# A conv and leaky-ReLU MLP on one core: the conv cut to 512-token blocks in three jobs a step, x cast on ScalarE, one transpose slot per block, and the first loads and casts set out anew

## Chip, cores and metric

One core of one Trainium2 chip. The metric is the device time of the kernel in microseconds; each time is one execution.

## What is computed

```python
# x (8, 4096, 192), weight (8 heads, 7 taps), w_in (192, 2048), w_out (2048, 192)
w = softmax(weight, axis=-1)
x_pad = zeros of 6 tokens in front of x, along the sequence
conv[b, s, h, g] = sum over k of w[h, k] * x_pad[b, s + k, h, g]   # 8 heads of 24 channels
a = conv.reshape(32768, 192)
h = a @ w_in
g = maximum(0.01 * h, h)
out = g @ w_out            # (32768, 192), float32
```

A causal depthwise convolution with seven taps, then two matrix products with a leaky ReLU between them.

## The kernel before

**Tiling.** Two sequences are worked at once, as two halves `e` of 64 partitions; the 192 channels are three chunks `c` of 64. A block is 512 tokens of both sequences, so there are 4 x 8 = 32 blocks. Each block passes through these stages: `load_x` (two DMAs on SP's queue, L72, 384 KB each, into one of three x_nat buffers), `cast_x` (float32 to bfloat16 on DVE, L85, two casts of 768 elements per partition), `transpose_x` (24 TensorE transposes of 64 rows, L101, into two PSUM tiles ptr0 and ptr1), `evac_x` (two DVE copies into the transposed sequence `xt`, L117), the conv (DVE, L134 for the first tap and L140 for the other six, per chunk), `mm1` (L242, six matmuls of 64 rows for each of 16 slices f of d_ff, the two sequences in the two row halves of the array), the leaky ReLU on ACT (Prelu, L249, 1024 elements), `mm2` (L260) and `evac_o` (a DVE copy out of PSUM, L303, and for every second one an output DMA on SP's queue, L306).

**Order.** The order of every engine's instructions is written out by hand. The main loop goes over 33 blocks and 8 steps j in each. A step of a block holds mm1 for two slices f with their Prelus, and the mm2 work of one 128-token output tile n of the block before (`n = (blk - 1) * 8 + j`): 16 matmuls of the upper row half for tile n, and 16 of the lower row half that run LAG = 24 matmuls, a step and a half, behind. So tile n-2 is finished in the middle of step n, and `evac_o(n-2)` is the first DVE work of that step. The lower half of a tile starts only behind the first Prelu of its step (`seal`). The last tiles are done with whole 128-row matmuls.

**PSUM.** `ph` has two slots of two banks. The tag `po` has four slots of one bank: the output sums take them, and the two transpose tiles ptr0 and ptr1 too, so a transpose needs an emptied sum's slot, and the next sum may get a transpose tile's slot.

**The conv.** It is made for units of two blocks (1024 tokens): 21 jobs of 1024 elements for a unit, spread over the 16 steps before it is needed; the first unit is done in pieces of 512.

**Preparation of later x.** In blocks 0 and 1, two blocks are prepared in each; from block 2 on, `prep(blk + 4, j, 1)` puts the load of blk+6 and the casts of blk+4 into step 1, and the transposes, one conv job and the xt copies into step 2:

```python
        if j == at:
            if blk + 2 < NBLK:
                load_x(blk + 2)
            cast_x(blk)
        if j == at + 1:
            transpose_x(blk)
            run_jobs(1)
            evac_x(blk)
```

**The start.** x of blocks 0 and 1 is loaded on SP's queue; the tap weights `wk` come in 20 small DMAs, half on POOL's queue and half on ACT's (L160); w_in (L171, two DMAs of 1536 KB, the same data for both partition halves) and w_out (L176, 1536 KB) follow on POOL's queue. 60 warm-up matmuls of 128 columns (L183) run early. The softmax of the taps (L191 to L206) comes ahead of the casts, transposes and copies of block 0 on DVE, then the conv of block 0. ACT casts w_in in four quarters (L221), then w_out (L226), and only then does its first Prelu.

Of the kernel before, what the change touches and what calls it, by code (L numbers as in the profile page):

```python
# [9 lines left out]
FP32 = mybir.dt.float32  # L10
BF16 = mybir.dt.bfloat16
# [3 lines left out]
def kernel(  # L15
# [8 lines left out]
    nc = tc.nc  # L24

    B, S, D = x.shape
    H, K = weight.shape
    Din, F = moe_w_in.shape
    GRP = D // H
# [8 lines left out]
    SUB = ST // 128  # L38
    NFC = F // 128
    NB = S // ST  # L40
    UB = 2
    UT = UB * ST
    NU = NB // UB
    NRP = B // 2
    NBLK = NRP * NB
    NUNIT = NRP * NU
    STEPS = 8
    FPS = NFC // STEPS

    const_pool = ctx.enter_context(tc.tile_pool(name="const", bufs=1))  # L50
# [11 lines left out]
    out_rows = out.rearrange("(r s) d -> r s d", r=B)  # L62


    x_nat = {}
    xt = {}

    def load_x(blk):
        rp, st = divmod(blk, NB)
# [10 lines left out]
    x_bf = {}  # L80

    def cast_x(blk):
        t = xb_pool.tile([128, SUB, NCH, 2, CH], BF16, name="x_bf")
        for e in range(2):
            nc.vector.tensor_copy(  # L85
                out=t[:, :, :, e, :],
                in_=x_nat[blk][:, e, :, :].rearrange("p s (c k) -> p s c k", c=NCH),
            )
        x_bf[blk] = t

    ptr = {}

    def transpose_x(blk):

# [10 lines left out]
                    )  # L105
        ptr[blk] = ts

    def evac_x(blk):
        rp, st = divmod(blk, NB)
        if st == 0:  # L110
            xt[rp] = xt_pool.tile([128, NCH, HALO + S], BF16, name="xt")
            nc.vector.memset(xt[rp][:, :, 0:HALO], 0.0)
        dst = xt[rp][:, :, HALO + st * ST : HALO + (st + 1) * ST].rearrange(
            "p c (s i k) -> p i s c k", s=SUB, i=2
        )
        for i, t in enumerate(ptr.pop(blk)):
            nc.vector.tensor_copy(out=dst[:, i], in_=t)  # L117


    yt = {}  # L120

    def conv_jobs(unit, pieces):
        rp, u = divmod(unit, NU)
        y = yt_pool.tile([128, NCH, UT], BF16, name="yt")
        yt[unit] = y
        jobs = []
        for o, n in pieces:
            for c in range(NCH):
                for k in range(K):
                    src = xt[rp][:, c, BASE + k + u * UT + o : BASE + k + u * UT + o + n]  # L130
                    dst = y[:, c, o : o + n]
                    if k == 0:
                        jobs.append(
                            lambda s=src, d=dst, c=c: nc.vector.tensor_scalar_mul(  # L134
                                d, s, wk[:, c, 0:1]
                            )
                        )
                    else:
                        jobs.append(
                            lambda s=src, d=dst, c=c, k=k: nc.vector.scalar_tensor_tensor(  # L140
                                out=d, in0=s, scalar=wk[:, c, k : k + 1], in1=d,
                                op0=mybir.AluOpType.mult, op1=mybir.AluOpType.add,
                            )
                        )
        return jobs

    load_x(0)
    load_x(1)


    wk = const_pool.tile([128, NCH, K], FP32, name="wk")
    for e in range(2):
        for c in range(NCH):
            lo = c * CH
            while lo < (c + 1) * CH:
                h = lo // GRP
                hi = min((h + 1) * GRP, (c + 1) * CH)
                p = e * CH + lo - c * CH
                eng = nc.gpsimd if e == 0 else nc.scalar
                eng.dma_start(  # L160
                    out=wk[p : p + hi - lo, c, :],
                    in_=weight[h : h + 1, :].to_broadcast((hi - lo, K)),
                )
                lo = hi
# [5 lines left out]
    for e in range(2):  # L170
        nc.gpsimd.dma_start(  # L171
            out=w_stage[e * CH : (e + 1) * CH, :, :],
            in_=moe_w_in.rearrange("(c p) f -> p c f", p=CH),
        )
    wo_stage = g_pool.tile([128, NFC, D], FP32, name="wo_stage", tag="g")
    nc.gpsimd.dma_start(  # L176
        out=wo_stage, in_=moe_w_out.rearrange("(c p) d -> p c d", p=128)
    )


    wa = psum_h.tile([128, 2, ST], FP32, name="warm", tag="ph")
    for i in range(60):
        nc.tensor.matmul(  # L183
            out=wa[:, 0, 0:128], lhsT=ident, rhs=ident,
            start=(i == 0), stop=(i == 59),
        )


    nmax = const_pool.tile([128, NCH], FP32)
    ssum = const_pool.tile([128, NCH], FP32)  # L190
    nc.vector.tensor_reduce(  # L191
        out=nmax, in_=wk, axis=mybir.AxisListType.X,
        op=mybir.AluOpType.max, negate=True,
    )
    for c in range(NCH):
        nc.scalar.activation(  # L196
            out=wk[:, c, :], in_=wk[:, c, :], func=mybir.ActivationFunctionType.Exp,
            bias=nmax[:, c : c + 1], scale=1.0,
        )
# [5 lines left out]
    for c in range(NCH):  # L205
        nc.vector.tensor_scalar_mul(wk[:, c, :], wk[:, c, :], ssum[:, c : c + 1])  # L206


    cast_x(0)
    transpose_x(0)  # L210
    evac_x(0)
    first = conv_jobs(0, [(0, ST), (ST, ST)])
    for job in first[: NCH * K]:
        job()
    cast_x(1)
    transpose_x(1)
    evac_x(1)

    w_in = const_pool.tile([128, NCH, F], BF16)
    for q in range(4):  # L220
        nc.scalar.copy(  # L221
            out=w_in[:, :, q * (F // 4) : (q + 1) * (F // 4)],
            in_=w_stage[:, :, q * (F // 4) : (q + 1) * (F // 4)],
        )
    w_out = const_pool.tile([128, NFC, D], BF16)
    nc.scalar.copy(out=w_out, in_=wo_stage)  # L226

    load_x(2)
    load_x(3)


    g = {}
    po = {}

    def mm1(blk, f):
        unit, ub = divmod(blk, UB)
        y = yt[unit]
        ph = psum_h.tile([128, 2, ST], FP32, name="ph", tag="ph")
        for c in range(NCH):
            for e in range(2):  # L240
# [1 line left out]
                nc.tensor.matmul(  # L242
                    out=ph[:, e, :],
                    lhsT=w_in[ps, c, f * 128 : (f + 1) * 128],
                    rhs=y[ps, c, ub * ST : (ub + 1) * ST],
                    start=(c == 0),
                    stop=(c == NCH - 1),
                )
# [29 lines left out]
    def mm2(n):  # L278
# [11 lines left out]
        if n >= LAST:  # L290
            for fc in range(NFC):
                mm2_one(None, n, fc)
            if n < NBLK * STEPS - 1:
                evac_o(n)

    def evac_o(n):
        blk, j = divmod(n, STEPS)
# [10 lines left out]
                in_=osb.pop(n // 2),  # L308
            )

    LAG = NFC + NFC // 2
    LAST = (NBLK - 1) * STEPS - 1
    osb = {}
    seal = {}
    jobs = list(first[NCH * K :])

    def prep(blk, j, at):
        if not blk < NBLK:
            return
        if j == at:  # L320
            if blk + 2 < NBLK:
                load_x(blk + 2)
            cast_x(blk)
        if j == at + 1:
            transpose_x(blk)
            run_jobs(1)
            evac_x(blk)

    def run_jobs(n):
        for _ in range(min(n, len(jobs))):  # L330
            jobs.pop(0)()

    for blk in range(NBLK + 1):
        unit, ub = divmod(blk, UB)
        if blk < NBLK:
            g[blk] = g_pool.tile([128, NFC, 2, ST], BF16, name="g", tag="g")
        for j in range(STEPS):
            n = (blk - 1) * STEPS + j
            if blk < NBLK:
# [3 lines left out]
                        seal[n] = act.ins.name  # L343
            if n >= 0:
                mm2(n)
            if blk == 0:
                prep(2, j, 0)
                prep(3, j, 4)
            elif blk == 1:
                prep(4, j, 0)  # L350
                prep(5, j, 4)
            else:
                prep(blk + 4, j, 1)
            if ub == 0 and j == (7 if blk == 0 else 0) and unit + 1 < NUNIT:
                jobs += conv_jobs(unit + 1, [(0, UT)])

            left = (7 - j) if blk == 0 and j < 7 else (UB - ub) * STEPS - j
            run_jobs(-(-len(jobs) // left))
    evac_o(NBLK * STEPS - 1)


# [28 lines left out]
```

## Time and profile before

| | |
|---|---|
| median of 3 runs | 757.04 us (756.85 to 759.33) |
| profiled execution | 757.87 us |
| its span | 756.1 us |
| TensorE matmul busy (PE) | 700.1 us, 93% |
| weight loads (PEld) | 565.5 us, 75% |
| VectorE (DVE) | 520.3 us, 69% |
| ScalarE (ACT) | 506.6 us, 67% |
| GpSimd (POOL) | 8.5 us |
| mean granted TensorE clock | 0.981 |
| HBM read, written | 29.90 MB, 25.17 MB |

The span is the time from the first to the last instruction; the execution's own time is 1.77 us more. The busy share is an average over a start, a long steady part and an end. PE counts a matmul from its start to its modelled end, so back-to-back matmuls overlap in it. In the rows shown below, `x12` counts instructions, and a name in brackets behind an idle time is what ended it; a group's row ends with its busy time, the mean nanoseconds of one instruction, and the idle time ahead of it with what ended that.

### The profile page before, as it was taken

What the parts mean: (1) busy time and instruction counts of PE and PEld (TensorE: products, weight loads), DVE (VectorE), ACT (ScalarE), POOL (GpSimd) and SP (SyncE); (2) the same over time, 40 slices, a digit from 0 to 9 for tenths busy, and PEclk for the clock granted to TensorE, in tenths of its full rate; (3) what the DMA queues carried; (4) which work ended last, traced back from release to release, by engine and by line L of the source; (5) the groups of instructions that cost most, each with busy time, mean ns of one, the idle gap of its engine ahead of it and who ended that gap; (6) DMA issues with size and microseconds to landing.
All of it is one profiled execution on the core that took longest, in us unless ns stands there. A gap on an engine that the chain in (4) does not pass through costs nothing.

```text
span 756.1 us, 25743 instructions
## 1 busy us (share of the span) xinstructions
PE 700.1 (93%) x11948; PEld 565.5 (75%) x11948; DVE 520.3 (69%) x752; ACT 506.6 (67%) x521; POOL 8.5 (1%) x19
## 2 busy tenths in 40 slices
PE   3178799999999999999999999999999999999997
PEld 3036578787877878787787878778787877888887
DVE  3979876867767687776768687676868677675112
ACT  1485567676777777676776767777676767777771
POOL 4000000000000000000000000000000000000000
PEclk9589999999999999999999999999999999999999
DMA  8921212222221222222122222221222211111112
GB/s 202 265 77 40 66 56 86 75 86 75 76 84 35 86 75 86 75 86 75 46 73 85 75 75 86 75 66 53 86 75 86 75 34 43 44 33 44 33 44 64
DMA packets 70131, 56.71 MB, mean 75 GB/s; under 512 B 3752, under 2 KB 69304, under 8 KB 69640
## 3 DMA queue, kind: packets, MB, share of 16 engines
q1 hardware_dynamic: 68608, 50.34, 22.0%
q0 software_dynamic: 1104, 4.73, 2.7%
q8 instruction: 93, 1.52, 0.8%
q14 instruction: 14, 0.11, 0.1%
q10 hardware_dynamic: 312, 0.01, 0.0%
HBM read 29.90 MB, written 25.17 MB: 73 GB/s over the span
## 4 chain that ended last, share of the span: by engine, by line
PE 81%; DVE 11%; DMA 3%; issue 3%; ACT 1%; POOL 0%; ACTq 0%; POOLq 0%
PE po L260 40%; PE ph L242 39%; DVE yt L140 7%; DMA w_stage<-in_moe_w_in_dram 3%; DVE x_bf L85 2%; PE ptr L101 2%; DVE o_sb L303 1%; ACT w_in L221 1%; DMA wk<-in_weight_dram 1%; DVE xt L117 1%; ACT w_out L226 0%; ACT g L249 0%; DVE yt L134 0%; POOL wk L160 0%; POOL w_stage L171 0%
## 5 line engine op out<-in xcount | busy, mean ns | idle before, releaser
L249 ACT ACTIVATE g<-ph 128x1024 bf16<-128x1024 f32 x512 | 496.4, 1021 | 204.9 <-PE ph L242 204.9
L260 PEld LDWEIGHTS <-g 64*128 64x128 bf16 (+1 forms) x8048 | 364.1, 94 | 47.2 <-issue 4.2
L242 PE MATMUL ph<-yt,w_in 64*128 64x512 bf16 x3072 | 388.7, 379 | 10.0 <-ACT g L249 4.9
L260 PE MATMUL po<-w_out,g 64*128 64x192 bf16 (+1 forms) x8048 | 391.6, 243 | 3.1 <-DVE xt L117 3.0
L140 DVE SCALAR_TENSOR_TENSOR yt<-xt,wk,yt 128x1024 bf16<-128x1024 bf16 (+1 forms) x306 | 371.8, 1215 | 3.5
L242 PEld LDWEIGHTS <-w_in 64*128 64x128 bf16 x3072 | 195.9, 95 | 97.0 <-issue 17.8
L303 DVE COPY o_sb<-po 128x192 f32<-128x192 f32 x256 | 90.9, 355 | 209.8 <-PE po L260 209.8
L101 PE MATMUL ptr<-ident,x_bf 64*128 64x64 bf16 x768 | 20.4, 193 | 30.3 <-DVE x_bf L85 17.3
L101 PEld LDWEIGHTS <-x_bf 64*128 64x128 bf16 x768 | 17.4, 97 | 33.6 <-DVE x_bf L85 17.9
L117 DVE COPY xt<-ptr 128x768 bf16<-128x768 bf16 x64 | 32.4, 547 | 7.0 <-PE ptr L101 7.0
L85 DVE CAST x_bf<-x_nat 128x768 bf16<-128x768 f32 x64 | 32.6, 551 | 0.0
L134 DVE TENSOR_SCALAR yt<-xt,wk 128x1024 bf16<-128x1024 bf16 (+1 forms) x51 | 23.6, 462 | 0.0
L221 ACT CAST w_in<-w_stage 128x1536 bf16<-128x1536 f32 x4 | 5.6, 1468 | 18.1 <-DMA w_stage<-in_moe_w_in_dram 18.1
L183 PE MATMUL warm<-ident 128*128 128x128 bf16 x60 | 6.2, 301 | 8.3 <-POOL ident masks.py:199 8.3
L183 PEld LDWEIGHTS <-ident 128*128 128x128 bf16 x60 | 6.0, 144 | 8.3 <-POOL ident masks.py:199 8.3
L191 DVE TENSOR_REDUCE nmax<-wk 128x3 f32<-128x21 f32 x1 | 0.2, 174 | 10.6 <-DMA wk<-in_weight_dram 10.6
L196 ACT ACT_TABLE_LOAD x1 | 1.3, 1283 | 7.6 <-DMA wk<-in_weight_dram 7.6
L160 POOL DMA_DIRECT2D wk<-in_weight_dram x10 | 5.3, 539 | 1.9 <-DMA wk<-in_weight_dram 1.1
L226 ACT CAST w_out<-wo_stage 128x3072 bf16<-128x3072 f32 x1 | 2.7, 2747 | 0.0
L196 ACT ACTIVATE wk<-wk,nmax 128x7 f32<-128x7 f32 x3 | 0.8, 301 | 2.0 <-DVE nmax L191 2.0
L171 POOL DMA_DIRECT2D w_stage<-in_moe_w_in_dram x2 | 1.3, 646 | 0.0
L176 POOL DMA_DIRECT2D wo_stage<-in_moe_w_out_dram x1 | 1.2, 1196 | 0.0
(11 smaller groups left out, 2.2 us busy)
## 6 DMA issues: line engine op xcount, KB each, us to landing
x_nat<-in_x_dram SPq DMA_DIRECT2D x64, 384.0 KB, 4.4
out_dram<-o_sb SPq DMA_DIRECT2D x128, 192.0 KB, 2.0
w_stage<-in_moe_w_in_dram POOLq DMA_DIRECT2D x2, 1536.0 KB, 17.0
wo_stage<-in_moe_w_out_dram POOLq DMA_DIRECT2D x1, 1536.0 KB, 25.5
wk<-in_weight_dram ACTq DMA_DIRECT2D x6, 0.7 KB
wk<-in_weight_dram POOLq DMA_DIRECT2D x6, 0.7 KB, 4.5
wk<-in_weight_dram ACTq DMA_DIRECT2D x2, 0.4 KB, 4.3
wk<-in_weight_dram ACTq DMA_DIRECT2D x2, 0.2 KB
```

Of the source, the lines that this page charges most:

```text
L85: nc.vector.tensor_copy(out=t[:, :, :, e, :], in_=x_nat[blk][:, e, :, :].rearrange("p s (c k) -> p s c k", c=NCH),)
L101: nc.tensor.transpose(out=ts[i][:, s, c, :], in_=x_bf[blk][ps, s, c, :, :].rearrange("p e k -> p (e k)"), identity=ident[ps, ps],)
L117: nc.vector.tensor_copy(out=dst[:, i], in_=t)
L134: lambda s=src, d=dst, c=c: nc.vector.tensor_scalar_mul(d, s, wk[:, c, 0:1])
L140: lambda s=src, d=dst, c=c, k=k: nc.vector.scalar_tensor_tensor(out=d, in0=s, scalar=wk[:, c, k : k + 1], in1=d, op0=mybir.AluOpType.mult, ...
L160: eng.dma_start(out=wk[p : p + hi - lo, c, :], in_=weight[h : h + 1, :].to_broadcast((hi - lo, K)),)
L183: nc.tensor.matmul(out=wa[:, 0, 0:128], lhsT=ident, rhs=ident, start=(i == 0), stop=(i == 59),)
L221: nc.scalar.copy(out=w_in[:, :, q * (F // 4) : (q + 1) * (F // 4)], in_=w_stage[:, :, q * (F // 4) : (q + 1) * (F // 4)],)
L242: nc.tensor.matmul(out=ph[:, e, :], lhsT=w_in[ps, c, f * 128 : (f + 1) * 128], rhs=y[ps, c, ub * ST : (ub + 1) * ST], start=(c == 0), stop ...
L249: return nc.scalar.activation(out=g[blk][:, f, :, :], in_=ph, func=mybir.ActivationFunctionType.Prelu, alpha=0.01,)
L260: ins = nc.tensor.matmul(out=po[m], lhsT=g[b][ps, fc, e, s * 128 : (s + 1) * 128], rhs=w_out[ps, fc, :], start=(rt != 1 and fc == 0), stop ...
L303: nc.vector.tensor_copy(out=o_sb[:, n % 2, :], in_=po.pop(n))
```

## The change

The conv is made block by block (512 tokens, 21 jobs), three jobs in each of steps 0 to 6 of the block before, with three `yt` buffers. From block 0 on every block prepares the one two ahead: the load of blk+3 stands in step 0, the casts of blk+2 are four half casts of 384 elements on ACT in steps 2 to 5, and the transposes and the xt copies stand in step 7. At the start, x of block 0 comes first and is cast half on DVE and half on ACT, transposed and copied before the softmax of the taps; block 1's casts and its copies out of PSUM are on ACT. `wk` comes in 14 DMAs over three queues. w_in comes in eight DMAs on SP's queue, behind x of blocks 0 and 1; w_out is one DMA on POOL's queue that casts to bfloat16, so its cast on ACT goes. An Exp on a dummy element loads ACT's table early. The warm-up becomes 56 matmuls of 512 columns and 64 rows, behind the transposes of block 1.

```diff
-    yt_pool = ctx.enter_context(tc.tile_pool(name="yt", bufs=2))
+    yt_pool = ctx.enter_context(tc.tile_pool(name="yt", bufs=3))
...
+    def cast_x(blk, e, copy, half=None):
+        if blk not in x_bf:
+            x_bf[blk] = xb_pool.tile([128, SUB, NCH, 2, CH], BF16, name="x_bf")
+        s = slice(0, SUB) if half is None else slice(half * SUB // 2, (half + 1) * SUB // 2)
+        copy(
+            out=x_bf[blk][:, s, :, e, :],
+            in_=x_nat[blk][:, e, s, :].rearrange("p s (c k) -> p s c k", c=NCH),
+        )
...
-    def evac_x(blk):
+    def evac_x(blk, copy):
...
-    def conv_jobs(unit, pieces):
-        rp, u = divmod(unit, NU)
-        y = yt_pool.tile([128, NCH, UT], BF16, name="yt")
+    def conv_jobs(blk):
+        rp, st = divmod(blk, NB)
+        y = yt_pool.tile([128, NCH, ST], BF16, name="yt")
...
+    queues = [nc.scalar, nc.gpsimd, nc.sync]
+    for i, (p, c, h, n, m) in enumerate(parts):
+        src = weight[h : h + n, :]
+        queues[i % 3].dma_start(
+            out=wk[p : p + n * m, c, :],
+            in_=bass.AP(tensor=src.tensor, offset=src.offset, ap=[[K, n], [0, m], [1, K]]),
+        )
+    load_x(1)
     w_stage = g_pool.tile([128, NCH, F], FP32, name="w_stage", tag="g")
...
+    for q in range(WQ):
+        for e in range(2):
+            fs = slice(q * F // WQ, (q + 1) * F // WQ)
+            nc.sync.dma_start(
+                out=w_stage[e * CH : (e + 1) * CH, :, fs],
+                in_=moe_w_in[:, fs].rearrange("(c p) f -> p c f", p=CH),
+            )
+    w_out = const_pool.tile([128, NFC, D], BF16)
+    nc.gpsimd.dma_start(out=w_out, in_=moe_w_out.rearrange("(c p) d -> p c d", p=128))
+    load_x(2)
...
+    junk = const_pool.tile([128, 1], FP32)
+    nc.vector.memset(junk, 0.0)
+    nc.scalar.activation(out=junk, in_=junk, func=mybir.ActivationFunctionType.Exp)
+
+    cast_x(0, 0, nc.vector.tensor_copy)
+    cast_x(0, 1, nc.scalar.copy)
+    transpose_x(0)
+    evac_x(0, nc.vector.tensor_copy)
...
+    for job in conv_jobs(0):
         job()
...
+    cast_x(1, 0, nc.scalar.copy)
+    cast_x(1, 1, nc.scalar.copy)
     transpose_x(1)
-    evac_x(1)
+    evac_x(1, nc.scalar.copy)
...
-    w_out = const_pool.tile([128, NFC, D], BF16)
-    nc.scalar.copy(out=w_out, in_=wo_stage)
...
+    NWARM = 56
+    for i in range(NWARM):
+        nc.tensor.matmul(
+            out=wa[:, 0, :], lhsT=ident[0:CH, :], rhs=xt[0][0:CH, 0, HALO : HALO + ST],
+            start=(i == 0), stop=(i == NWARM - 1),
+        )
...
+        jobs = conv_jobs(blk + 1) if blk + 1 < NBLK else []
         for j in range(STEPS):
...
-            if blk == 0:
-                prep(2, j, 0)
-                prep(3, j, 4)
-            elif blk == 1:
-                prep(4, j, 0)
-                prep(5, j, 4)
-            else:
-                prep(blk + 4, j, 1)
...
+            if blk + 2 < NBLK:
+                if j == 0:
+                    load_x(blk + 3)
+                if 2 <= j < 6:
+                    cast_x(blk + 2, j % 2, nc.scalar.copy, half=(j - 2) // 2)
+                if j == 7:
+                    transpose_x(blk + 2)
+                    evac_x(blk + 2, nc.vector.tensor_copy)
+            for job in jobs[3 * j : 3 * (j + 1)]:
+                job()
```

More of the change, by code (lines that the diff above doesn't have):

```diff
@@ L62 @@
     out_rows = out.rearrange("(r s) d -> r s d", r=B)
-    x_nat = {}
-    xt = {}
+    x_nat, x_bf, xt, ptr = {}, {}, {}, {}
     def load_x(blk):
+        if blk >= NBLK:
+            return
         rp, st = divmod(blk, NB)
@@ L116, in evac_x @@
         for i, t in enumerate(ptr.pop(blk)):
[L117 removed]
+            copy(out=dst[:, i], in_=t)
     yt = {}
[L122 to L125 removed]
+    def conv_jobs(blk):
+        rp, st = divmod(blk, NB)
+        y = yt_pool.tile([128, NCH, ST], BF16, name="yt")
+        yt[blk] = y
         jobs = []
[L127 to L136, printed above, removed]
[L137 to L143 removed]
@@ L181 @@
[L181 to L186, printed above, removed]
+    wk = const_pool.tile([128, NCH, K], FP32, name="wk")
+    parts = []
+    for c in range(NCH):
+        lo = c * CH
+        while lo < (c + 1) * CH:
+            h = lo // GRP
+            n = 1
+            hi = min((h + 1) * GRP, (c + 1) * CH)
+            if lo == h * GRP:
+                while (h + n + 1) * GRP <= (c + 1) * CH:
+                    n += 1
+                    hi = (h + n) * GRP
+            parts += [(e * CH + lo - c * CH, c, h, n, (hi - lo) // n) for e in range(2)]
+            lo = hi
@@ L204 @@
     nc.vector.reciprocal(ssum, ssum)
[L205 to L213, printed above, removed]
+    nc.vector.tensor_mul(wk, wk, ssum.unsqueeze(2).to_broadcast((128, NCH, K)))
+    for job in conv_jobs(0):
         job()
-    cast_x(1)
+    cast_x(1, 0, nc.scalar.copy)
+    cast_x(1, 1, nc.scalar.copy)
     transpose_x(1)
-    evac_x(1)
+    evac_x(1, nc.scalar.copy)
     w_in = const_pool.tile([128, NCH, F], BF16)
[L220 to L223, printed above, removed]
-        )
-    w_out = const_pool.tile([128, NFC, D], BF16)
[L226 to L233, printed above, removed]
+    for q in range(WQ):
+        fs = slice(q * F // WQ, (q + 1) * F // WQ)
+        nc.scalar.copy(out=w_in[:, :, fs], in_=w_stage[:, :, fs])
+    wa = psum_h.tile([128, 2, ST], FP32, name="warm", tag="ph")
+    NWARM = 56
[3 more added lines that the diff above has]
+            start=(i == 0), stop=(i == NWARM - 1),
+        )
+    g, po, osb, seal = {}, {}, {}, {}
     def mm1(blk, f):
-        unit, ub = divmod(blk, UB)
-        y = yt[unit]
+        y = yt[blk]
         ph = psum_h.tile([128, 2, ST], FP32, name="ph", tag="ph")
```

101 lines of the change are left out of this document (24 added, 77 removed).

## The prediction

> **What bounds the kernel now.** I read the page's shares first, then the chain that ended last cut to the first 90 us, then TensorE's timeline block by block, then the engines that feed it.
>
> ```profile
> span 756.1 us, 25743 instructions
> PE 700.1 (93%) x11948; PEld 565.5 (75%) x11948; DVE 520.3 (69%) x752; ACT 506.6 (67%) x521; POOL 8.5 (1%) x19
> ```
>
> The chain over the first 90 us (start, length, what):
>
> ```profile
> 8.86 20.83 DMA w_stage<-in_moe_w_in_dram
> ...
> 35.36 2.65 ACT w_out L226
> 38.98 2.74 PE ph L242 x12
> 43.40 0.67 DVE yt L140
> ...
> 86.54 1.04 PE ph L242 x8
> ```
>
> In this stretch nothing is bound by TensorE: up to 38.0 the start waits for w_in's load and then for ACT, which casts w_in and w_out, and from 43.4 to 86.5 DVE is behind with the conv. Only from 86.5 on is TensorE the bound, and 93% hides that. TensorE's timeline shows what a block costs there (a block begins with its first L242 row):
>
> ```profile
> 173.49 1.50 PE L242 MATMUL ph<-yt,w_in 64*128 64x512 bf16 x12
> 178.72 1.53 PE L242 MATMUL ph<-yt,w_in 64*128 64x512 bf16 x12
> ...
> 182.46 0.51 PE L101 MATMUL ptr<-ident,x_bf 64*128 64x64 bf16 x23 [0.89 <-DVE o_sb L303]
> 195.90 1.48 PE L242 MATMUL ph<-yt,w_in 64*128 64x512 bf16 x12
> 201.13 1.51 PE L242 MATMUL ph<-yt,w_in 64*128 64x512 bf16 x12
> 203.74 0.51 PE L101 MATMUL ptr<-ident,x_bf 64*128 64x64 bf16 x22
> 217.19 1.50 PE L242 MATMUL ph<-yt,w_in 64*128 64x512 bf16 x12
> 654.48 1.50 PE L242 MATMUL ph<-yt,w_in 64*128 64x512 bf16 x12
> 675.40 1.53 PE L242 MATMUL ph<-yt,w_in 64*128 64x512 bf16 x12
> 736.38 1.53 PE L242 MATMUL ph<-yt,w_in 64*128 64x512 bf16 x12
> ```
>
> A plain step is 2.615 us (two from 173.49 to 178.72). A block without transposes is 20.92 (654.48 to 675.40), an odd block with them 21.29 (195.90 to 217.19), so 24 transposes cost 0.37; an even block is 22.41 (173.49 to 195.90), 1.12 more: all but the first of its transposes wait for an o_sb copy (x23). The last row is the last step of block 31, which ends at 739.0. DVE's timeline says why the copy is late in an even block and not in an odd one:
>
> ```profile
> 178.34 0.36 DVE L303 COPY o_sb<-po 128x192 f32<-128x192 f32 x1 [0.58 <-PE po L260]
> 178.61 1.02 DVE L85 CAST x_bf<-x_nat 128x768 bf16<-128x768 f32 x2
> ...
> 182.06 0.35 DVE L303 COPY o_sb<-po 128x192 f32<-128x192 f32 x1
> 203.34 0.36 DVE L303 COPY o_sb<-po 128x192 f32<-128x192 f32 x1 [0.93 <-PE po L260]
> ```
>
> Between 178.61 and 182.06 DVE makes two casts and two conv jobs of 1024, more than a step, and the copy starts 3.34 after its step's first L242 (178.72). When DVE was idle it starts 2.21 after (203.34 less 201.13), and its bank is free just as the transposes arrive, at 203.74.
>
> **The change, part by part: the blocks.** po has four slots. At a step's end two hold open sums, and the two transpose tiles take those of sums n-3 and n-2, the last of them emptied by the o_sb copy of this very step. There are still 24 transposes a block, now behind step 7, so TensorE saves nothing but the wait, and what decides is whether step 7's copy is on time. The casts leave DVE; in step 6 it has one copy, then three jobs of 512, priced by:
>
> ```profile
> 16.02 0.35 DVE L134 TENSOR_SCALAR yt<-xt,wk 128x512 bf16<-128x512 bf16 x1
> 21.02 0.35 DVE L134 TENSOR_SCALAR yt<-xt,wk 128x512 bf16<-128x512 bf16 x1
> 43.31 2.31 DVE L140 SCALAR_TENSOR_TENSOR yt<-xt,wk,yt 128x512 bf16<-128x512 bf16 x3
> 45.55 0.35 DVE L134 TENSOR_SCALAR yt<-xt,wk 128x512 bf16<-128x512 bf16 x1
> L140 DVE SCALAR_TENSOR_TENSOR yt<-xt,wk,yt 128x1024 bf16<-128x1024 bf16 x270 | 344.8, 1277 | 2.4
> ```
>
> A copy holds DVE for 0.27 (178.34 to 178.61), three dependent jobs for 2.24 (43.31 to 45.55): 2.51 of a 2.615 step in steps 1, 3, 5 and 6, and some 0.4 less in steps 0, 2 and 4, which hold a cheap multiply. So each copy finds DVE free with 0.1 to spare, and the stall goes. The small jobs make DVE's conv dearer, not cheaper: the 18 long ones of a block were 11.5 (9 of 1.277) and are 13.4 (six times 2.24); seven jobs take 5.0 (16.02 to 21.02), a block's conv 15.0. With 8 copies (2.2) and two xt copies (1.0, as the two casts) DVE has 18.2 of a block's 21.29, and the conv ends ahead of step 7's copy. The xt copies come right behind the transposes, step 7 having no jobs, and the next po, which takes a transpose tile's slot, has the step's first matmuls (half a step, 1.3) as cover. Next to be late is step 7's copy again, if a job of 512 takes 0.03 more than here. The third yt slot and the later place of the transposes cost nothing: each conv reads what was copied a block before.
>
> ACT takes four half casts of 384 elements in steps 2 to 5, behind the step's two Prelus.
>
> ```profile
> L221 ACT CAST w_in<-w_stage 128x1536 bf16<-128x1536 f32 x4 | 5.6, 1468 | 18.1 <-DMA w_stage<-in_moe_w_in_dram 18.1
> L226 ACT CAST w_out<-wo_stage 128x3072 bf16<-128x3072 f32 x1 | 2.7, 2747 | 0.0
> 44.86 6.83 ACT L249 ACTIVATE g<-ph 128x1024 bf16<-128x1024 f32 x7 [0.16 <-PE ph L242]
> 179.64 1.94 ACT L249 ACTIVATE g<-ph 128x1024 bf16<-128x1024 f32 x2 [0.68 <-PE ph L242]
> ```
>
> 1279 ns for 1536 more elements are 0.833 ns each, so 384 take 0.19 + 0.32 = 0.51, about 0.41 of it in the open (two Prelus take 1.94, a tenth less than twice one). The gap ahead of the next step's first Prelu is 0.68: hidden. Without that cover the Prelu is late, and with it the matmuls of the second row half, which wait for it through `seal`. Bounds: 0.41, and, for the cut-up strides, the 1.02 of a Prelu over 1024; the plain casts are nearest, so 0.51. On SP the load of block + 3 stands at step 0, behind an output DMA, more than a block ahead of its casts: nothing.
>
> **The head.** Stretches (the last columns: granted clock, DMA share, GB/s) and loads:
>
> ```profile
> 0.00:5.00 5.00, 0.00 (x0) 0.00 (x0) 0.00 (x0) 0.00 (x0) 3.92 (x11) 1.00 0.54 163
> 5.00:10.00 5.00, 1.68 (x16) 1.68 (x17) 0.00 (x0) 1.28 (x1) 3.84 (x9) 1.00 0.64 171
> 20.00:25.00 5.00, 0.00 (x0) 0.00 (x0) 4.79 (x8) 0.00 (x0) 0.00 (x0) 0.50 1.04 224
> 30.00:35.00 5.00, 2.93 (x36) 1.53 (x37) 4.05 (x9) 5.00 (x4) 0.00 (x0) 0.50 1.08 326
> 40.00:45.00 5.00, 5.00 (x49) 2.33 (x46) 2.56 (x5) 3.21 (x4) 0.00 (x0) 0.54 0.03 9
> x_nat<-in_x_dram SPq DMA_DIRECT2D x64, 384.0 KB, 4.4
> w_stage<-in_moe_w_in_dram POOLq DMA_DIRECT2D x2, 1536.0 KB, 17.0
> wo_stage<-in_moe_w_out_dram POOLq DMA_DIRECT2D x1, 1536.0 KB, 25.5
> L183 PE MATMUL warm<-ident 128*128 128x128 bf16 x60 | 6.2, 301 | 8.3 <-POOL ident masks.py:199 8.3
> 12.69 1.02 DVE L85 CAST x_bf<-x_nat 128x768 bf16<-128x768 f32 x2
> ```
>
> *Loads.* The bytes stay, their order changes. x0 and x1 (1.57 MB) took the first 10 us (163 and 171 GB/s make 1.67 MB). w_in moves at 224 GB/s: 3.15 MB, 14.0 us. w_out's 1.57 MB at 326 GB/s are 4.8 us, and now share the engines with x1 and w_in instead of coming last. Its cast inside the DMA no row shows. Below: nothing, if it fits the 4.1 us in which the DMA stood idle in the first 10 (0.46 and 0.36 of 5). Above: twice 4.8. Nearest is the plain load, half of it in the idle time, 2.4. So w_in's bytes are in at 10 + 2.4 + 14.0 = 26.4; a landing comes up to 3.2 later (x's 4.4 less the 1.2 that its bytes need), I add 2: 28.4, between 24 and 34. The last quarter's cast, 1.5, makes 29.9. SP now issues 18 loads in a row, some of which POOL and ACT issued; all but the last are queued before their turn. w_out's 2.65 on ACT goes; the table load, now ahead of x's cast, falls where ACT idles.
>
> *Conv of block 0.* It started at 16.02, 3.3 behind the end of wk's chain (12.69), with x's casts, transposes and copies in between. These now come first: 12.7 at the latest, ended by 27.7.
>
> *Warm-up.* 60 matmuls of 128 columns took 6.15 us, so 512 take 0.41 at the low clock; a plain step's 2.615 hold 6144 columns, 0.218 for 512 at the full one. The clock came at about 44.6 (the mean of 0.54 in that stretch), 5.6 after the run that began at 38.98: 13.7 slow ones and 42.3 fast ones, 14.8 us. By the Trainium skill, "TensorE: Matmul & The Clock Gate", Part 1, some 3.4 us of sustained work open the clock; an estimate by that is 13.8, and the sum 1 us less. It starts once x1 has come (10, or 15 if it waits behind w_out), was cast on ACT (two of 0.83) and transposed (0.8): 12.5 to 17.5, and ends at 27.3 to 32.3. The first Prelu comes 0.9 later and behind w_in's casts: 29.9 to 33.2. I take 31.5, against 38.0.
>
> *Block 0* is then ACT's: 16 Prelus at 0.968 (6.83 less 1.02, by six) and four casts at 0.41, 17.2. Block 1 enters one Prelu before the last ends: 31.5 + 17.2 - 1.0 = 47.7. Its conv, 15.0 behind the first, is done by 43. Block 1 takes 21.29 and 0.3 of waiting for block 0's last Prelu. Block 2 begins at 69.3; before, it could run only from 86.5.
>
> **The sum.** 69.3; blocks 2 to 29, with transposes, 28 x 21.29 = 596.1; blocks 30 and 31, 41.8; from 739.0 to the end, unchanged, 17.1: 724.3 against 756.1. Of the 31.8, some 14 are stalls inside the blocks and 18 the head. The profiled execution took 757.87, 1.77 over its span, and the median of the runs, 757.04, is 0.83 below that: 725.2.
>
> **The rivals.** (1) The warm-up never gets the full clock, its matmuls filling half the rows: 56 x 0.41 = 23.0, first Prelu at up to 41.4, time 735. For it: TensorE was cold from 20 on. Against it: L242's tiles have 64 rows too, if two at a time, and the clock came. 0.09. (2) The head gains nothing, because w_in's last quarter sits in SP's queue until block 2 starts as late as before: 757 less 14, 743. Against it: ACT's 2.65 and DVE's lag are gone whatever the loads do. 0.05. (3) The stall stays in a new place: step 7's copy is late by 1.12 in 28 blocks, 31 us, 756, no change. For it: 0.1 of spare. Against it: step 6 would have to take DVE 3.6 us; a miss of 0.1 costs 0.1 a block. 0.04. (4) Slower: a half cast doesn't fit ACT's gap. Each 0.1 us over 0.75 delays four steps in 30 blocks, 12 us; at 1.02 all that was gained is lost, and at 1.1 the time is 767. The Trainium skill, "ScalarE: Activation LUTs", Rules for kernel authors, wants simple elementwise work on VectorE rather than ScalarE, which speaks for this case. Against it: 0.83 ns an element on ACT stand against 0.66 on DVE (1.02 for two of 768). 0.03.
>
> **How the numbers follow.** The forecast has 0.79. Its own range is 719 to 732: a first Prelu between 28.2 and 35.5 gives 722 to 729, and 0.1 a block either way 3 more. The range goes on to (1), 718 to 737. A measurement of this kernel tells 0.3%, 2.3 us, from no change. Faster holds the forecast, (1) and (2): 0.93; same is (3), 0.04; slower (4), 0.03.
>
> **What would show it.** Right: no wait of L101 for o_sb, blocks of 21.3, no conv in the chain behind 50 us, the first Prelu near 31. Wrong: TensorE idle ahead of the transposes; a cast on ACT with no gap behind it; a granted clock of 0.5 beyond 30 us; w_stage landing after 34.

## The result, and the profile after

The changed kernel takes 740.31 us in the median of 4 runs (739.89 to 740.75), the kernel before 758.18 (4 runs): a ratio of 0.976, with an interval of 0.974 to 0.979. It is faster, but by 18 us instead of 32, and 740 lies outside the range of 718 to 737. The profiled execution took 740.75; its span is 738.9, against 724.3 in the sum. All of the 14.6 us between the two lie ahead of the first Prelu.

From the page of the profile: the shares, a DMA queue (packets, MB, share of the DMA engines' time), a group and a load.

```profile
span 738.9 us, 26161 instructions
PE 712.5 (96%) x11944; PEld 608.2 (82%) x11944; DVE 567.0 (77%) x1002; ACT 555.1 (75%) x644; POOL 5.0 (1%) x12
...
q0 software_dynamic: 2224, 0.80, 1.0%
...
L221 PE MATMUL warm<-xt,ident 64*128 64x512 bf16 x56 | 24.1, 631 | 0.0
...
w_out<-in_moe_w_out_dram POOLq DMA_DIRECT2D x1, 768.0 KB, 12.6
```

PE has 12 us more than before: the warm-up alone is 24.1, where it was 6.2. The chain that ended last, cut to the first 70 us (start, length, what):

```profile
6.78 0.57 SPq L71
...
7.40 11.94 DMA x_nat<-in_x_dram
...
19.36 0.84 ACT x_bf L83
...
20.25 0.82 PE ptr L96 x21
21.07 23.87 PE warm L221 x56
44.94 2.44 PE ph L235 x6
```

x of block 1 is issued only at 6.78 and 7.40 and is in at 19.34; the warm-up stands behind its transposes and holds TensorE to 44.94. ACT shows what waits for that:

```profile
33.36 1.47 ACT L215 CAST w_in<-w_stage 128x1536 bf16<-128x1536 f32 x1 [2.20 <-DMA w_stage<-in_moe_w_in_dram]
46.29 4.08 ACT L242 ACTIVATE g<-ph 128x1024 bf16<-128x1024 f32 x4 [11.46 <-PE warm L221]
```

ACT had w_in cast at 34.8 and then waited 11.46 us for the warm-up. The first Prelu is at 46.29; the prediction had 31.5, a miss of 14.8, which is the miss of the span.

From there on the trace is the one predicted. TensorE's timeline (first matmuls of block 1, 2, and two steady blocks):

```profile
62.33 1.74 PE L235 MATMUL ph<-yt,w_in 64*128 64x512 bf16 x12
83.86 1.47 PE L235 MATMUL ph<-yt,w_in 64*128 64x512 bf16 x12
254.35 1.46 PE L235 MATMUL ph<-yt,w_in 64*128 64x512 bf16 x11
272.61 1.53 PE L235 MATMUL ph<-yt,w_in 64*128 64x512 bf16 x12
275.23 0.53 PE L96 MATMUL ptr<-ident,x_bf 64*128 64x64 bf16 x22
275.65 1.46 PE L235 MATMUL ph<-yt,w_in 64*128 64x512 bf16 x11
296.96 1.46 PE L235 MATMUL ph<-yt,w_in 64*128 64x512 bf16 x11
```

Each block takes 21.31 us (254.35 to 275.65 to 296.96), and the even ones no longer 22.41. The transposes come 2.62 us behind their step's first matmul (272.61 to 275.23), one plain step, with no wait. DVE and ACT in the same stretch:

```profile
272.23 0.36 DVE L295 COPY o_sb<-po 128x192 f32<-128x192 f32 x1
272.50 2.32 DVE L134 SCALAR_TENSOR_TENSOR yt<-xt,wk,yt 128x512 bf16<-128x512 bf16 x3
274.84 0.36 DVE L295 COPY o_sb<-po 128x192 f32<-128x192 f32 x1
```

```profile
262.28 0.51 ACT L83 CAST x_bf<-x_nat 128x384 bf16<-128x384 f32 x1
263.07 1.94 ACT L242 ACTIVATE g<-ph 128x1024 bf16<-128x1024 f32 x2 [0.28 <-PE ph L235]
```

Step 7's copy starts 2.23 behind its step's first matmul, where it started 3.34 behind in the kernel before. A half cast takes 0.51 on ACT and leaves 0.28 of its gap.

### The profile page after: what moved, and what is told of

Read it like the earlier page. It is cut to its first block, busy times and chain, and to the rows that moved or that the text cites. A ratio compares the mean times of both kernels' runs of the same rounds, so it can differ in the third digit from the quotient of the medians.

```text
span 738.9 us, 26161 instructions
## 1 busy us (share of the span) xinstructions
PE 712.5 (96%) x11944; PEld 608.2 (82%) x11944; DVE 567.0 (77%) x1002; ACT 555.1 (75%) x644; POOL 5.0 (1%) x12
## 3 DMA queue, kind: packets, MB, share of 16 engines
q1 hardware_dynamic: 70368, 53.49, 23.9%
## 4 chain that ended last, share of the span: by engine, by line
PE 95%; DMA 2%; ACT 2%; ACTq 0%; issue 0%; SPq 0%; DVE 0%
PE po L253 46%; PE ph L235 44%; PE warm L221 3%; ACT g L242 2%; DMA x_nat<-in_x_dram 2%; PE ptr L96 2%; DMA wk<-in_weight_dram 1%; ACT x_bf L83 0%; ACTq L163 0%; SPq L71 0%; SPq L163 0%; DVE o_sb L295 0%
## 5 line engine op out<-in xcount | busy, mean ns | idle before, releaser
L134 DVE SCALAR_TENSOR_TENSOR yt<-xt,wk,yt 128x512 bf16<-128x512 bf16 x576 | 431.2, 749 | 14.0
L253 PEld LDWEIGHTS <-g 64*128 64x128 bf16 (+1 forms) x8048 | 374.9, 94 | 32.4 <-issue 0.2
L253 PE MATMUL po<-w_out,g 64*128 64x192 bf16 (+1 forms) x8048 | 399.2, 243 | 0.0
L235 PE MATMUL ph<-yt,w_in 64*128 64x512 bf16 x3072 | 395.1, 377 | 3.3 <-ACT g L242 2.7
L235 PEld LDWEIGHTS <-w_in 64*128 64x128 bf16 x3072 | 233.3, 94 | 59.6 <-issue 9.5
L83 ACT CAST x_bf<-x_nat 128x384 bf16<-128x384 f32 (+1 forms) x123 | 64.1, 521 | 3.7 <-DMA x_nat<-in_x_dram 3.7
L128 DVE TENSOR_SCALAR yt<-xt,wk 128x512 bf16<-128x512 bf16 x96 | 33.2, 346 | 0.1
L221 PE MATMUL warm<-xt,ident 64*128 64x512 bf16 x56 | 24.1, 631 | 0.0
L221 PEld LDWEIGHTS <-ident 64*128 64x128 bf16 x56 | 8.2, 147 | 15.0 <-issue 15.0
L83 DVE CAST x_bf<-x_nat 128x768 bf16<-128x768 f32 x1 | 0.7, 657 | 3.6 <-DMA x_nat<-in_x_dram 3.6
```

The costliest lines, as they stand in the source:

```text
L83: copy(out=x_bf[blk][:, s, :, e, :], in_=x_nat[blk][:, e, s, :].rearrange("p s (c k) -> p s c k", c=NCH),)
L128: lambda s=src, d=dst, c=c: nc.vector.tensor_scalar_mul(d, s, wk[:, c, 0:1])
L221: nc.tensor.matmul(out=wa[:, 0, :], lhsT=ident[0:CH, :], rhs=xt[0][0:CH, 0, HALO : HALO + ST], start=(i == 0), stop=(i == NWARM - 1),)
L235: nc.tensor.matmul(out=ph[:, e, :], lhsT=w_in[ps, c, f * 128 : (f + 1) * 128], rhs=y[ps, c, :], start=(c == 0), stop=(c == NCH - 1),)
L253: ins = nc.tensor.matmul(out=po[m], lhsT=g[b][ps, fc, e, s * 128 : (s + 1) * 128], rhs=w_out[ps, fc, :], start=(rt != 1 and fc == 0), stop ...
```

## The experiments

What had to be settled: why the warm-up ran at the low clock to its end, what held x1 and w_in, and whether it is the casts on ACT that removed the stall. In all tables of windows the granted clock reads 1.00 in the first 47 us of the changed kernel, for which the trace holds no record of the clock: its first record is of the full clock, from 47.08 us on. So the clock is read below from the pace of the matmuls, start to start: 0.427 us for 512 columns (23.87 over 56) is the low one, 0.216 to 0.218 the full one.

### The warm-up

**e1_warm_128rows.** The same 56 matmuls over all 128 rows.

```diff
-            out=wa[:, 0, :], lhsT=ident[0:CH, :], rhs=xt[0][0:CH, 0, HALO : HALO + ST],
+            out=wa[:, 0, :], lhsT=ident, rhs=xt[0][:, 0, HALO : HALO + ST],
```

> The warm-up's 56 matmuls of 512 columns take 128 rows (whole identity, both halves of xt) instead of 64; nothing else is changed. In the changed kernel they ran at 0.427 us each from 20.9 to 44.9, and the first Prelu was at 46.3. Theory A (a stream through only 64 rows does not open the clock): the clock opens some 5.6 us after 20.9, the warm-up takes 14 to 15 us and ends near 35.5, the first Prelu is at 36.5 (w_in's last cast ends at 34.8), the time 730.5. Rival B (the data: half an identity is mostly zeros) and rival C (the place in the program, or one long accumulation into one bank): no change, 740.3.

Measured: 730.34 us (730.04 to 730.86), 0.962 of before (0.960 to 0.964). TensorE, and ACT's first Prelus:

```profile
22.05 12.98 PE L221 MATMUL warm<-xt,ident 128*128 128x512 bf16 x53 [0.22 <-issue]
34.97 1.47 PE L235 MATMUL ph<-yt,w_in 64*128 64x512 bf16 x12
...
35.83 5.81 ACT L242 ACTIVATE g<-ph 128x1024 bf16<-128x1024 f32 x6 [1.23 <-PE ph L235]
```

The warm-up ran from 21.22 to 34.97, 13.75 us: 7.8 matmuls at 0.427 and 48.2 at 0.216, so the clock opened after some 3.3 us. The trace's first record of the clock, full from 24.39 on, puts it at 3.2.

**e2_warm_pairs.** 112 matmuls of 64 rows, by turns in the upper and the lower half of the array, each half into a bank of its own.

```diff
-    NWARM = 56
+    NWARM = 112
...
+            out=wa[:, i % 2, :],
+            lhsT=ident[i % 2 * CH : (i % 2 + 1) * CH, :],
+            rhs=xt[0][i % 2 * CH : (i % 2 + 1) * CH, 0, HALO : HALO + ST],
```

> The warm-up as 112 matmuls of 64 rows that alternate between the two row halves, into two banks, as mm1 does it: the same stream time if they run in pairs. Theory A (rows at work in total): as with 128 rows, 730.5, first Prelu at 36.5. If instead each matmul counts by its own 64 rows, the clock stays low: 740.3, or 764 if they also don't pair.

**e4_warm_dense64.** The 64 rows of the change, with x itself as the stationary tile in place of the identity.

```diff
-            lhsT=ident[0:CH, :]
+            lhsT=xt[0][0:CH, 1, HALO : HALO + 128]
```

> The warm-up keeps 64 rows, but its stationary operand is 64 x 128 of xt instead of half an identity: dense data. Theory A (rows): no change, 0.427 us each, first Prelu at 46.3, 740.5. Rival B (data): the clock opens, first Prelu at 36.5, 730.5.

Measured: the pairs 730.07 us, dense data in one half 740.98 us (one run each). TensorE's timelines, the pairs first:

```profile
21.12 14.04 PE L221 MATMUL warm<-xt,ident 64*128 64x512 bf16 x112
```

```profile
21.00 23.23 PE L221 MATMUL warm<-xt 64*128 64x512 bf16 x54
```

112 paired matmuls take 14.04 us and 54 single ones 23.23. So it is the rows that the stream fills. The zeros of the identity are not the cause, as dense data in one half (e4) changed nothing, and neither are the number of matmuls, their place or the single bank that they write, as e1 shares all three. The changed kernel's own trace agrees:

```profile
43.49 0.60 PE L235 MATMUL ph<-yt,w_in 64*128 64x512 bf16 x1
```

mm1, which works in both halves, starts at 43.49 beside the last of the warm-up, and the clock is recorded as full from 47.08 on, 3.6 us later. No run shows whether one half would open the clock in more than 23.9 us, or whether the other half alone differs.

The Trainium skill, "TensorE: Matmul & The Clock Gate", Part 1, states that about 3.4 us of sustained work bring the full clock, at a point that varies because the window runs freely. The runs with filled rows lie around that: worked out as above, 3.3 in e1, 3.6 in e2, and 2.8, 3.0 and 3.8 in e8, e9 and e12 below, with 5.3 in e11 well behind it. The stream through 64 rows does not agree: 23.9 us of unbroken matmuls never got the clock.

**e3_no_warm.** The warm-up is left out.

> No warm-up at all. The first Prelu is then bound by w_in's last cast, 34.9. mm1 of block 0 starts cold: three pairs at 0.427 are 1.28 a slice against ACT's 0.97, until the clock opens; between 5.6 us (4 slices, 1.5 us lost) and 10 us (2.5 us lost). Theory A, the warm-up is pure delay: 730 to 733. Rival (the warm-up does shorten what follows): 740 or more.

Measured: 729.9 us (729.41 to 730.02), 0.961 of before (0.960 to 0.963). ACT:

```profile
32.57 1.47 ACT L215 CAST w_in<-w_stage 128x1536 bf16<-128x1536 f32 x1 [1.97 <-DMA w_stage<-in_moe_w_in_dram]
33.95 1.93 ACT L233 ACTIVATE g<-ph 128x1024 bf16<-128x1024 f32 x2
```

The warm-up of the change cost 10.4 us and bought nothing. One that opens the clock (e1) costs 1.9 us at the first Prelu (35.83 against 33.95) and gives most of it back as faster first steps: 730.3 against 729.9. What is left of the miss, 33.95 against 31.5, is the loads: w_in's last cast starts at 32.57 where the prediction had 28.4.

### The loads

**e5_x1_first.** e3 with the load of x1 right behind that of x0.

```diff
     load_x(0)
+    load_x(1)
...
-    load_x(1)
     w_stage = g_pool.tile([128, NCH, F], FP32, name="w_stage", tag="g")
```

> Without the warm-up, so that the loads decide, and x of block 1 issued on SP's queue right behind x of block 0, ahead of the four small wk loads. In the changed kernel its second half was issued at 7.4 and landed at 19.3. Theory D (SP's queue made x1 late, it sat behind wk loads that waited): x1 lands by 10, w_in follows 4 us earlier, the first Prelu is at 30 instead of 34, the time 726. Rival E (w_out's casting transfer holds the engines whoever is ahead): x1 still lands after 15, the time 729.9 as without warm-up alone.

**e6_wout_late.** e3 with w_out's load held back until w_in is in: a POOL copy of one column from w_in's staging into w_out, which the load then overwrites.

```diff
+    nc.gpsimd.tensor_copy(out=w_out[:, 0, 0:1], in_=w_stage[:, 0, F - 1 : F])
     nc.gpsimd.dma_start(out=w_out, in_=moe_w_out.rearrange("(c p) d -> p c d", p=128))
```

> Without the warm-up, and w_out's casting load made to wait for the last quarter of w_in (a one-column copy on POOL from w_stage into w_out ahead of it). Issue order on SP's queue is unchanged. Theory E: x1 lands at 12 to 13, the last wk load before 9, w_in's last quarter at 27 to 28 instead of 32.6, the first Prelu is at 29.5, the time 725; w_out lands at 40, ahead of block 1. Theory D: x1 no earlier than 17, the time 729.9.

Measured: e5 731.49 us, e6 724.25 us (one run each). First e5, DVE:

```profile
19.04 0.17 DVE L192 TENSOR_REDUCE nmax<-wk 128x3 f32<-128x21 f32 x1 [9.99 <-DMA w_stage<-in_moe_w_in_dram]
```

Then e6, DVE and ACT:

```profile
8.96 0.17 DVE L193 TENSOR_REDUCE nmax<-wk 128x3 f32<-128x21 f32 x1
...
12.45 0.83 ACT L83 CAST x_bf<-x_nat 128x768 bf16<-128x768 f32 x1 [0.64 <-DMA x_nat<-in_x_dram]
27.00 1.47 ACT L216 CAST w_in<-w_stage 128x1536 bf16<-128x1536 f32 x1 [2.27 <-DMA w_stage<-in_moe_w_in_dram]
```

With x1 put first, the small loads of wk are the ones that wait: the softmax of the taps, which reads wk alone, starts at 19.04 (14.16 in the changed kernel, 13.82 in e3). ACT casts x1 only behind its Exp of that softmax, at 19.59, so the early load gains nothing, and the run is 1.6 us slower than e3: neither D's time nor E's came. With w_out out of the way everything is early: wk 8.96, x1 12.45 (19.36 with the change), w_in 27.00 (32.57), and 5.6 us come off e3. So w_out's load is what delays the rest, and changing the order of what shares the engines with it only moves the delay. The Trainium skill, "DMA: Bandwidth & Descriptors", Queues, rings and completion order, says that the DMA engines are shared by all queues and take turns between them packet by packet; a load on POOL's queue that delays SP's loads by 5.6 us agrees.

**e10_plain_wout.** e3 with w_out loaded early as plain float32 and cast on ACT, to tell the cast inside the DMA from the bytes.

```diff
-    nc.gpsimd.dma_start(out=w_out, in_=moe_w_out.rearrange("(c p) d -> p c d", p=128))
+    nc.gpsimd.dma_start(out=wo_stage, in_=moe_w_out.rearrange("(c p) d -> p c d", p=128))
...
+    nc.scalar.copy(out=w_out, in_=wo_stage)
```

> Without the warm-up; w_out loaded early on POOL's queue as in the changed kernel, but plain in float32, and cast on ACT behind w_in's casts as in the kernel before (2.65 us ahead of the first Prelu). It asks whether the cast inside the transfer or the 1.57 MB as such held x1, wk and w_in back. Theory H (the casting transfer is slow and holds the engines): w_out is through by 12 or 13, x1 lands by 15, w_in's last quarter by 28.5, the first Prelu is at 32.5 in spite of the cast, the time 728. Rival I (any w_out of that size ahead of them does it): x1 at 19, w_in at 32.5, the first Prelu at 36.6, the time 732.5.

Measured: 730.96 us (one run). Page and ACT:

```profile
q0 software_dynamic: 528, 1.58, 0.7%
...
wo_stage<-in_moe_w_out_dram POOLq DMA_DIRECT2D x1, 1536.0 KB, 9.2
```

```profile
30.80 1.47 ACT L215 CAST w_in<-w_stage 128x1536 bf16<-128x1536 f32 x1 [1.75 <-DMA w_stage<-in_moe_w_in_dram]
32.17 2.75 ACT L217 CAST w_out<-wo_stage 128x3072 bf16<-128x3072 f32 x1
```

w_in's last cast starts at 27.00 without w_out, at 30.80 behind the plain load in packets of 3 KB, at 32.57 behind the casting one in packets of 360 bytes: 3.8 us come with the bytes and 1.8 with the casting form, of which no run tells the cast from the small packets. The second is the less certain: in six runs with the change's own loads (the changed kernel, e1 to e4 and e7) the same cast starts between 32.21 and 33.36. Neither expectation holds alone, and the bytes weigh more. The cast on ACT then costs 2.75, and e10 is 1.1 us slower than e3.

### The stall

**e7_casts_dve.** The changed kernel with the half casts of the loop on DVE.

```diff
-                    cast_x(blk + 2, j % 2, nc.scalar.copy, half=(j - 2) // 2)
+                    cast_x(blk + 2, j % 2, nc.vector.tensor_copy, half=(j - 2) // 2)
```

> The changed kernel with one edit: the four half casts of a block are on DVE instead of ACT, in the same steps 2 to 5. Block 0 loses 1.7 us on ACT. Theory F (what removed the stall is that no step of DVE exceeds 2.615 us): steps 3 and 5 grow to 2.8 (a half cast is some 0.27), the copy of step 7 is late by about 0.1, blocks are 21.4, the time 741 (740.3 + 2 - 1.7). Rival G (the move of the casts off DVE is the gain by itself): the 1.12 stall comes back, blocks of 22.4, the time 770.

Measured: 739.25 us (one run). DVE and TensorE:

```profile
268.06 0.36 DVE L295 COPY o_sb<-po 128x192 f32<-128x192 f32 x1
268.34 0.35 DVE L83 CAST x_bf<-x_nat 128x384 bf16<-128x384 f32 x1
268.60 2.32 DVE L134 SCALAR_TENSOR_TENSOR yt<-xt,wk,yt 128x512 bf16<-128x512 bf16 x3
270.84 0.35 DVE L295 COPY o_sb<-po 128x192 f32<-128x192 f32 x1
...
273.34 0.35 DVE L295 COPY o_sb<-po 128x192 f32<-128x192 f32 x1
```

```profile
271.08 1.52 PE L235 MATMUL ph<-yt,w_in 64*128 64x512 bf16 x12
273.69 0.58 PE L96 MATMUL ptr<-ident,x_bf 64*128 64x64 bf16 x24
```

Step 5 takes DVE 2.78 (268.06 to 270.84), 0.17 more than a step, and step 6, with no cast, 2.50. The copy ahead of the transposes starts 2.26 behind its step's first matmul, and the transposes a plain step behind it: no stall. So the casts' move to ACT is not needed for the gain in the blocks, and theory F's account stands, without the small delay that it priced. The gain goes with steps that never load DVE by more than a step for long, and with a step 6, the last ahead of the transposes, that has slack; no run parts the smaller conv jobs from the later place of the transposes, so which of the two is needed stays open. Moving the casts back takes four of them off ACT in block 0; the run is 1.1 us shorter, which one run hardly tells.

### Together

**e8_all_three.** 48 warm-up matmuls of 128 rows, x1 first, w_out late. **e9_best.** The 48 matmuls, w_out late, x1 where the change has it, casts on DVE. **e11_best_58.** e9 with 58.

> Three edits together: a warm-up of 48 matmuls over 128 rows, x of block 1 ahead of the wk loads on SP's queue, and w_out's load behind w_in's last quarter. If theories A, D and E all hold, x1 lands by 10, the warm-up runs from 13 to 26 at the open clock, w_in's last quarter lands at 25 to 26, the first Prelu is at 27.5, block 2 begins 18.8 before the changed kernel's 83.9 and the time is 721.5. If the loads are bound by their bytes alone (x0, x1 and w_in at 334 and 224 GB/s from 2 us on end at 21) it could be 718; if only A holds, 730.

> A version that should beat both: a warm-up of 48 matmuls over 128 rows, w_out's load behind w_in's last quarter, the half casts on DVE; x of block 1 stays behind the wk loads. Against the run with w_out late and no warm-up (724.3): the cold matmuls of block 0 go (about 2.5 us of 27.7, some of it hidden), and ACT's four casts of block 0 (1.5). First Prelu at 28.5, the time 721. If the warm-up (from 14.2, 11.8 us long) is late again or the casts matter on DVE, 724 or more.

> The version before this one with one number changed: 58 warm-up matmuls instead of 48. There the warm-up ended at 25.4, two slices of mm1 followed, then TensorE stood idle for 3.1 us behind ACT's last w_in cast, and the next 24 matmuls took 4.6 us where 24 at the full clock take 2.9 to 3.5. If the idle time took the clock away, ten more matmuls (2.2 us) shorten it to about 1 us, the clock stays, four slices take 0.3 us less each and the time is 1 us less, 721. If those matmuls were slow for another reason, 722.

Measured: e8 723.69 us (723.00 to 726.25), 0.954 of before (0.951 to 0.957); e9 722.03 (720.24 to 722.98), 0.951 (0.948 to 0.953); e11 722.40 (721.86 to 722.80), 0.953 (0.952 to 0.955). e8 missed its 721.5 by 2.2 us: with x1 first, wk's softmax starts at 12.28 (8.80 in e9) and w_in's last cast at 28.38 (27.44 in e9); the first Prelu, expected at 27.5, follows that cast at 29.76. TensorE's wait of 1.36 us for the conv in its first step lies ahead of this and does not set it. In e9 the clock came and went again, and the trace records it as low from 30.00 to 33.41; TensorE, and a stretch (granted clock 0.63 behind ACT's and POOL's columns):

```profile
13.49 11.92 PE L222 MATMUL warm<-xt,ident 128*128 128x512 bf16 x48
29.89 4.62 PE L236 MATMUL ph<-yt,w_in 64*128 64x512 bf16 x24 [3.07 <-ACT g L243]
```

```profile
29.89:34.50 4.61, 4.61 (x24) 1.80 (x24) 4.50 (x9) 3.67 (x4) 0.00 (x0) 0.63 1.35 263
```

Between its first 12 matmuls of mm1 and the next TensorE waits 3.07 us for ACT, and then 24 matmuls take 4.62, 0.193 each, where pairs at the full clock take 0.109 (half of 0.218). e11 fills that gap, but its clock came 2 us later, the warm-up took 15.21 and the first Prelu is at 29.65 instead of 28.82: nothing gained.

**e12_wk_two_queues.** e9 with wk's loads on ACT's and POOL's queues only.

```diff
-    queues = [nc.scalar, nc.gpsimd, nc.sync]
+    queues = [nc.scalar, nc.gpsimd]
...
-        queues[i % 3].dma_start(
+        queues[i % 2].dma_start(
```

> The run e9 with the tap weights on ACT's and POOL's queues only (7 DMAs each), none on SP's. In e9 SP's four wk issues hold SP from 1.76 to 6.65, so x of block 1 is issued only at 6.67 and w_in from 7.84 on, while the DMA engines are half idle from 5 to 10 us (0.30 busy in that stretch of the run e6). J: the late issue is what w_in pays; x1 and w_in are issued 4.9 us earlier, w_in lands some 3 us earlier (24.4 instead of 27.4), first Prelu near 26, time 719 (e9: 722.0). K: the loads queued ahead make wk land late instead, as in the run with x1 first (wk at 12.0 in e8, 8.0 in e9), and the conv of block 0, 15 us behind wk's softmax, becomes the last: wk at 12 to 14, conv done at 29 to 31, first Prelu 29.5 to 31.5, time 722.5 to 724.5.

Measured: 720.56 us (720.18 to 721.62), 0.950 of before (0.947 to 0.953), the lowest median here. SP's queue, ACT and TensorE:

```profile
0.74 7.30 SPq L71 DMA_DIRECT2D x_nat<-in_x_dram  x4
8.09 5.97 SPq L172 DMA_DIRECT2D w_stage<-in_moe_w_in_dram  x8
```

```profile
27.93 4.89 ACT L243 ACTIVATE g<-ph 128x1024 bf16<-128x1024 f32 x5
```

```profile
29.00 1.74 PE L236 MATMUL ph<-yt,w_in 64*128 64x512 bf16 x12 [1.09 <-ACT g L243]
```

Neither theory held. wk's loads came later but still in time (the softmax starts at 10.24, 8.80 in e9), and w_in's first issue is at 8.09 (7.84 in e9): SP issues three x loads by 2.3 and the fourth only at 7.67. So it is not wk's issues that hold SP, and what does (its fourth issue waits in every run here, the kernel before included: 6.09) stays open. In the trace the first Prelu is 0.9 earlier than in e9 and the clock holds over a gap of 1.09 us.

A gain over e9 is not shown. The median is 1.5 us lower, but the ranges overlap (e9's shortest run took 720.24), and against the kernel before, timed beside each, e9 stands at 0.951 and e12 at 0.950. The runs go with their mean granted clock: e9's two at 0.997 took 722.74 and 722.98, its two at 0.999 and 1.000 took 721.32 and 720.24; e12's one at 0.997 took 721.62, the three at 1.000 took 720.18 to 720.66. That fits a clock that is lost in the start of some runs of a kernel and not in others, though only one run of each has a trace.

## Why the prediction was right and wrong

**Blocks: right to 0.02 us.** 21.31 for 21.29. From block 2's start to the end 655.04 (738.9 less 83.86) for 655.0 (724.3 less 69.3). DVE's 2.51 of a step with 0.1 to spare: 2.61 and 2.62 from copy to copy, which is the step's own pace, and no stall. ACT's half cast: 0.51 in the trace, and of the 0.68 gap the 0.41 in the open leave 0.27, where 0.28 is seen. Rivals (3) and (4) did not happen, and e7 shows that the casts would have fitted on DVE too. Block 0 from the first Prelu: 16.04 (46.29 to 62.33) for 16.2; block 1: 21.53 for 21.6.

**The warm-up: the step that failed.** 23.87 us for 14.8. The price took the moment at which the clock opened in the kernel before from the run that began at 38.98. Those are mm1's tiles: 64 rows, but always two at once in the two halves. The warm-up fills one half alone. The text saw the difference (rival (1): "if two at a time") and gave it 0.09; e2 against e4 is that difference measured, 14.0 against more than 23. What the trace of before did show, tiles in both halves, bore on e2's case and not on the change's. The other stream that got the clock there, the warm-up that starts at 8.32 (full clock recorded from 13.88, 5.6 us later), filled all 128 rows. That warm-up's 0.41 was also a little low, as the mean took in its last seven matmuls, which ran at the full clock; the low pace is 0.427. The estimate of 13.8, from 3.4 us of sustained work, fell with the same step.

**The loads: too early.** w_in was to be in at 28.4, and its last cast starts at 33.36 (32.57 in e3). Three terms are behind it. x1, "10, or 15 if it waits behind w_out", came at 19.34. w_out's load was priced at 2.4, "half of it in the idle time", between nothing and 9.6: it is 5.6 (e3 against e6), inside the bounds, with the point taken too low. That "all but the last are queued before their turn" is wrong for x1: with x0 and part of wk issued, SP gets to x1 at 6.78. Even with w_out late x1 is in at 12.4 and not at 10, and from 5 to 10 us the DMA engines of the changed kernel moved only 54 GB/s:

```profile
0.00:5.00 5.00, 0.00 (x0) 0.00 (x0) 0.62 (x2) 0.27 (x1) 4.10 (x12) 1.00 0.58 158
5.00:10.00 5.00, 0.82 (x24) 0.67 (x24) 1.15 (x4) 1.93 (x3) 0.90 (x1) 1.00 0.60 54
```

By the shares, 0.58 and 0.60, the DMA engines stood idle for 4.1 us of these ten, as in the kernel before, so the idle time that was to hide half of w_out was not used. Without w_out the sum's 10 + 14.0 + 2 = 26.0 for w_in stands against 26.9 in e6, where x1 came 2.4 later than the 10 of the sum: w_in's bytes and rate were sound to about a microsecond, in part because w_in was issued from 8.42 on, while x1 was still coming. The conv of block 0, "12.7 at the latest", began at 15.69, as wk's loads, too, stood behind w_out; it was not the last to be ready (the profile names x_nat as what the softmax waited for, but the softmax reads wk alone, whose last load on SP's queue landed at 13.65):

```profile
14.16 0.17 DVE L192 TENSOR_REDUCE nmax<-wk 128x3 f32<-128x21 f32 x1 [5.29 <-DMA x_nat<-in_x_dram]
15.69 0.35 DVE L128 TENSOR_SCALAR yt<-xt,wk 128x512 bf16<-128x512 bf16 x1
```

**How the 14.8 divide.** With a warm-up that opens the clock the first Prelu is at 35.83 (e1): 10.5 of the 14.8 are the clock, 4.3 the loads. Either alone would have left the time within the range: the loads alone are e1, at 730.3; the clock alone was not run, and rival (1) put it at up to 735. Rival (1) at 735 was the case that came, and missed by 5 because it let the warm-up start at 17.5 at the latest (it started at 21.07) and at 0.41 a matmul (0.427). The range ended at 737 because it added the two errors' bounds nowhere: (1)'s worst start was the forecast's.

**The signs that were named.** "The first Prelu near 31" did not come, and "TensorE idle ahead of the transposes" did not appear. w_stage was in by 33.4, so "w_stage landing after 34" did not appear either. The sign "a granted clock of 0.5 beyond 30 us" could not have shown the failure: that column reads 1.00 in five microseconds that 13 matmuls of 512 columns, the first and last cut off, fill:

```profile
25.00:30.00 5.00, 5.00 (x13) 1.78 (x12) 4.79 (x8) 1.78 (x2) 0.00 (x0) 1.00 1.08 208
```

## What to carry to other kernels

When a duration is taken over from one row to another, compare the forms of the two, rows and halves of the array included: the clock that opened under paired tiles said nothing of a stream through one half, and a warm-up that does not open it is pure delay in front of the first real matmul. In the start of a kernel price a load by what the loads beside it lose, and look at when the queue gets to issue each one; holding w_out back until w_in was in gave 5.6 us here, for one small copy. In the steady part look at the load of the feeding engine in the step just ahead of the handover: here the stall was gone once that step had slack, and it mattered little which engine the casts were on.

## What the runs showed of the hardware that was not expected

- 23.9 us of back-to-back matmuls over 64 rows left TensorE at 0.427 us for 512 columns, with an identity and with dense data; the same over 128 rows, or 64-row tiles by turns in both halves, got 0.216 after 2.8 to 5.3 us (e1, e2, e8, e9, e11, e12).
- In the traces an idle time of 3.07 us took the clock back (e9) and one of 1.09 did not (e12). It may not be so in every run: the mean granted clock of e9's runs is 0.997 in two, 0.999 and 1.000 in the others.
- An early load of 1.57 MB on POOL's queue delayed the other queues' loads by 3.8 us at w_in as a plain load and by 5.6 as a casting one. Read off the softmax, it held the small loads of wk from 8.96 (e6) to 13.82 (e3), and to 19.04 where x1 was put ahead of them (e5).
- SP's third issue came at 1.8 us in every run, its fourth only at 4.2 to 7.7, whether it was a load of wk or of x; the cause is open.
